# The head of a fused linear-attention and Mish kernel, rebuilt: roots on ScalarE, the wv load on ScalarE's queue, a value tile between fold and logits, eight PSUM banks, one ones column

## The chip, the cores and the metric

The kernel runs on one core of a Trainium2 chip. The metric is the device time of one execution in microseconds (us). Three runs of the kernel before took 184.01, 184.12 and 184.20 us; the median is 184.12.

The engines are called TensorE (PE in the profile; its weight loads are PEld), VectorE (DVE), ScalarE (ACT), GpSimd (POOL) and SyncE (SP). SP and ScalarE also issue the transfers (SPq, ACTq).

## The reference, cut to what matters

One input x of 2048 rows and 512 columns is normalised and goes into two branches, whose results are added to x.

```python
x = A_x
xn = _layernorm(x, axis=-1)
return x + _A_ref(xn, A_wqkv, A_w_phi, A_wo) + _B_ref(xn, B_w1, B_b1, B_w2)

def _A_ref(x, wqkv, w_phi, wo):                       # 32 heads of 16
    q, k, v = ...                                     # x @ wqkv, split
    pq = jnp.einsum("bhsd,hdf->bhsf", q, w_phi)
    pk = jnp.einsum("bhsd,hdf->bhsf", k, w_phi)
    phi_q = jnp.concatenate([_softmax(pq), _softmax(-pq)], axis=-1)
    phi_k = jnp.concatenate([_softmax(pk), _softmax(-pk)], axis=-1)
    kv = jnp.einsum("bhsf,bhsd->bhfd", phi_k, v)
    z  = jnp.einsum("bhsf->bhf", phi_k)
    num = jnp.einsum("bhqf,bhfd->bhqd", phi_q, kv)
    den = jnp.einsum("bhqf,bhf->bhq", phi_q, z)[..., None] + 1e-6
    return (num / den) @ wo                           # heads joined again

def _B_ref(x, w1, b1, w2):                            # F = 1792
    h = x @ w1 + b1
    return (h * jnp.tanh(softplus(h))) @ w2           # Mish
```

## The kernel before, in words

Rows are worked on in 16 tiles of 128, in four groups of four. Nothing is scheduled by a planner: the text of the kernel is the order of each engine's work (`manual_schedule`), and every engine takes its own list from the front. The order was written out by hand.

**The head** (L419 to L491) prepares the first group.

- Loads. SP's queue issues x tiles 0 and 1, the k part of wqkv turned by a DMA transpose (`wT`, `load_turned`, L90), x tiles 4 to 7, `wv`, `w1`, x tiles 8 to 15. ScalarE's queue issues `wsrc` (w_phi), x tiles 2 and 3, `b1b`.
- GpSimd builds `ident` and the block mask `block`; VectorE makes `KVmask` and the mask columns of `kvm` from it (L443 to L445).
- TensorE runs twelve matmuls on the identity (`warm`, L455) while nothing else can run.
- `ln_stats` (L116 to L122): VectorE takes the statistics of two tiles and aggregates them; GpSimd makes the reciprocal root from the variance (add, then power -0.5). `ln_apply` (L128) normalises on VectorE.
- `fold` (L98): TensorE multiplies `wT` with `Wbd`, the block-diagonal w_phi that VectorE builds (L461). The four slices of the result are evicted to `wkp`, three by ScalarE (L108), one by VectorE (L106).
- `ln_turn_pe` (L140): TensorE transposes a normalised tile into PSUM (`ptr`), one copy (L143) brings it to `xnT`.
- `logits(0, i)`: four matmuls `xnT` by `wkp` (L156), evicted to `p_sb` by ScalarE (L194). All four tiles' logits are done before the first `value(i)`, which multiplies by `wv` (L156) and is evicted to `vext` (L164).
- `extremes(0)` on VectorE (L207 to L218): maximum and minimum over each 16 of `p_sb`, and the differences `e`. In its middle it normalises tiles 4 to 7 and has their transposes done by DMA (L146).
- `hidden(5)`: five units of the first layer of the Mish branch, each four matmuls (L176) and one activation with the Mish table on ScalarE (L183). There are 56 such units in all, put between the other steps to fill TensorE.

**The loop over four groups**, s = 0 to 3: exponentials of `e` (L228, with a change of ScalarE's table before and after), `accumulate(s-1)` (L281: `pkv` += e' x `vext`, 32 matmuls), value and logit tiles of the next groups, `normalise` on VectorE (L246 to L259), more hidden units (6 + 11, 14, 8, 10), then `extremes(s+1)`. In group 0 three logit tiles go into one PSUM tile of three banks (`wide`, evicted at L531), and after that VectorE clears `pkv` (L533).

**After the loop:** the exponentials of the first query group, `accumulate(3)`, `mask_kv` (L294 to L307), and then per half group: `attend` (L325; evicted by ScalarE, L334 to L341), `combine` on VectorE (L357 to L382), a DMA transpose of its result `ob` (L385), `second_layer` (L398), `project_out` (L407), the residual and the store (L415, L416).

**PSUM** has eight banks. One pool of five (`ps`, tag `mm`) serves the matmul results of the head and of the loop; one of three banks (`ps2`) holds in turn `wide`, `pkv` and each `pnd` of `attend`.

`vext` holds, beside the 128 columns of v for eight heads, eight columns of ones (128 to 135), from which `pkv` gets the sums z in eight equal columns.

Of the kernel before, what the change touches and what calls it, by code (L numbers as in the profile page):

```python
# [17 lines left out]
def kernel(  # L18
# [12 lines left out]
    nc = tc.nc  # L31
    P = 128
    S, D, NH, DH, F = 2048, 512, 32, 16, 1792
    NG = 4
    TPG = 4
# [24 lines left out]
    ps2 = ctx.enter_context(tc.tile_pool(name="ps2", bufs=1, space=bass.MemoryType.PSUM))  # L60

    x_sb = persist.tile([P, NT, D], BF16, name="x_sb")
    xnT = persist.tile([P, NT, KT, P], BF16, name="xnT")
# [11 lines left out]
    wqp = wqk[:, :, 0:D]  # L75
    wo_sb = wqk[:, :, D : 2 * D]
    ident = consts.tile([P, P], BF16, name="ident")
    mhalf = consts.tile([P, TPG], FP32, name="mhalf")
    block = consts.tile([P, 8, 16], BF16, name="block")
    KVmask = consts.tile([P, 136], FP32, name="KVmask")  # L80
# [29 lines left out]
    def ln_stats(t0, n):  # L110

        stats = lnp.tile([P, TPG, nc.vector.BN_STATS_DIM], FP32, name="stats")
        mv = lnp.tile([P, TPG, nc.vector.BN_AGGR_DIM], FP32, name="mv")
        rstd = lnp.tile([P, TPG], FP32, name="rstd")
        for i in range(n):
            nc.vector.bn_stats(stats[:, i, :], x_sb[:, t0 + i, :])  # L116
        for i in range(n):
            nc.vector.bn_aggr(mv[:, i, :], stats[:, i, :])
        nc.gpsimd.tensor_scalar(
            out=rstd[:, 0:n], in0=mv[:, 0:n, 1], scalar1=1e-5, scalar2=None, op0=ALU.add  # L120
        )
        nc.gpsimd.tensor_tensor(out=rstd[:, 0:n], in0=rstd[:, 0:n], in1=mhalf[:, 0:n], op=ALU.pow)  # L122
        return mv, rstd

    def ln_apply(t0, n, mv, rstd, xn, at):
        engine = nc.gpsimd if t0 > TPG else nc.vector
        for i in range(n):
            engine.tensor_scalar(  # L128
                out=xn[:, at + i, :],
                in0=x_sb[:, t0 + i, :],  # L130
                scalar1=mv[:, i, 0:1],
                scalar2=rstd[:, i : i + 1],
                op0=ALU.subtract,
                op1=ALU.mult,
            )

    def ln_turn_pe(t, xn, i, copy):
        ptr = ps.tile([P, 512], BF16, name="ptr", tag="mm")
        for kt in range(KT):
            nc.tensor.transpose(  # L140
                ptr[:, kt * P : (kt + 1) * P], xn[:, i, kt * P : (kt + 1) * P], ident[:]
            )
        copy(xnT[:, t, :, :], ptr[:].rearrange("p (k c) -> p k c", k=KT))  # L143
# [18 lines left out]
    def value(t, copy):  # L162
        pv = project(wv, t)
        copy(  # L164
            vext[(t // TPG) % 2][:, t % TPG, :, 0:128], pv.rearrange("p (j c) -> p j c", j=4)
        )
# [108 lines left out]
    def accumulate(g):  # L275
        pkv = kv_of[0]
        e = e_of.pop(g)
        for j in range(4):
            for pl in range(2):
                for i in range(TPG):  # L280
                    nc.tensor.matmul(  # L281
                        blocks(pkv, pl, j, 136),
                        lhsT=e[:, i, pl, j * P : (j + 1) * P],
                        rhs=vext[g % 2][:, i, j, :],
                        start=False,
                        stop=(g == NG - 1 and i == TPG - 1),
                        skip_group_check=True,
                    )

    def mask_kv():  # L290
        pkv = kv_of[0]

        a, b = by_parts(pkv, 0, 136)
        nc.vector.tensor_tensor(  # L294
            out=kvm[:, :, 0:3, 0:136], in0=a,
            in1=KVmask[:, None, None, :].to_broadcast([P, 2, 3, 136]), op=ALU.mult,
        )
        nc.vector.tensor_tensor(
            out=kvm[:, :, 3, 0:136], in0=b,
            in1=KVmask[:, None, :].to_broadcast([P, 2, 136]), op=ALU.mult,  # L300
        )
        a, b = by_parts(pkv, 128, 136)
        nc.vector.scalar_tensor_tensor(
            out=kvm[:, 1, 0:3, 128:136], in0=a[:, 1], scalar=1e-6,
            in1=KVmask[:, None, 128:136].to_broadcast([P, 3, 8]), op0=ALU.add, op1=ALU.mult,
        )
        nc.vector.scalar_tensor_tensor(  # L307
            out=kvm[:, 1, 3, 128:136], in0=b[:, 1], scalar=1e-6,
            in1=KVmask[:, 128:136], op0=ALU.add, op1=ALU.mult,
        )  # L310

    nd_of, oT_of, po_of, tmp_of = {}, {}, {}, {}
# [103 lines left out]
        queue.dma_start(o_v[:, t, c], y)  # L416


    nc.sync.dma_start(x_sb[:, 0:2, :], x_v[:, 0:2, :])  # L419
    with nc.allow_non_contiguous_dma(reason="tiny w_phi load"):  # L420
        nc.scalar.dma_start(wsrc[:], wphi_v)
    wT = load_turned(D)
    nc.scalar.dma_start(x_sb[:, 2:4, :], x_v[:, 2:4, :])
    nc.scalar.dma_start(b1b[:], b1_v[:, :])
    nc.sync.dma_start(x_sb[:, 4:8, :], x_v[:, 4:8, :])
    nc.sync.dma_start(wv[:], wqkv_v[:, :, 2 * D : 3 * D])
    nc.sync.dma_start(w1_sb[:], w1_v[:, :, :])
    nc.sync.dma_start(x_sb[:, 8:16, :], x_v[:, 8:16, :])

# [13 lines left out]
    nc.vector.tensor_copy(KVmask[:, 0:P], block[:].rearrange("p h d -> p (h d)"))  # L443
    nc.vector.tensor_copy(KVmask[:, P : P + 8], block[:, :, 0])
    nc.vector.tensor_copy(  # L445
        kvm[:].rearrange("p l j c -> p (l j) c")[:, :, 136:144],
        block[:, None, :, 0].to_broadcast([P, 8, 8]),
    )
# [1 line left out]

    dve, act = nc.vector.tensor_copy, nc.scalar.copy

    warm = ps.tile([P, 4, P], FP32, name="warm", tag="mm")
    for _ in range(12):
        nc.tensor.matmul(  # L455
            warm[:], lhsT=ident[:], rhs=ident[:, None, :].to_broadcast([P, 4, P]),
            start=True, stop=True,
        )

    st0 = ln_stats(0, 2)  # L460
    nc.vector.tensor_tensor(  # L461
        out=Wbd[:].rearrange("p j (h e) -> p j h e", h=8),
        in0=block[:, None, :, :].to_broadcast([P, 4, 8, 16]),
        in1=wsrc[:, :, None, :].to_broadcast([P, 4, 8, 16]),
        op=ALU.mult,
    )
    st1 = ln_stats(2, 2)
    xn = lnp.tile([P, TPG, D], BF16, name="xn", tag="xn")
    ln_apply(0, 2, *st0, xn, 0)
    fold(wT, wkp, (3,))  # L470
    ln_turn_pe(0, xn, 0, dve)
    ln_turn_pe(1, xn, 1, act)
    pb = ps.tile([P, 512], BF16, name="pb", tag="mm")
    nc.tensor.transpose(pb[:, 0:FT], b1b[:], ident[0:FT, 0:FT])
    ln_apply(2, 2, *st1, xn, 2)
    logits(0, 0, act)
    for i in range(2, 4):
        ln_turn_pe(i, xn, i, dve)
    nc.vector.tensor_copy(b1f[:], pb[:, 0:FT])
    for i in range(1, TPG):  # L480
        logits(0, i, act)

    def normal(t0, st, xn):
# [6 lines left out]
    extremes(0, lambda: normal(TPG, st, xn))  # L490
    nc.sync.dma_start(w2_sb[:], w2_v[:, :, :])  # L491
    nc.sync.dma_start(wo_sb, wo_v[:, :, :])
    for i in range(TPG):
        value(i, act)
    hidden(5)

    for s in range(NG):
        exponentials(s, (0, 1) if s else (0,))
        if s > 0:
            accumulate(s - 1)  # L500
        if s < NG:
# [112 lines left out]
```

## Time and profile before

| | us |
|---|---|
| median of three runs | 184.12 |
| the profiled execution | 183.97 |
| its span in the profile | 182.3 |
| PE busy | 175.2 |
| DVE busy | 147.6 |
| ACT busy | 126.7 |
| POOL busy | 25.0 |

The span begins with the first instruction of the profile and ends with the last; 1.67 us of the execution lie outside of it. All times in the text are counted from the start of the span. "Busy" counts the time that an engine's instructions were being executed. Matmuls overlap in it: one of 512 columns is listed with some 379 ns, but in a stream they start 216 ns apart. "Waits" are idle times of an engine, put down to whatever was released last before the idle time ended. In a timeline row the first number is the start and the second the time to the end of the last instruction of the row; a bracket names the idle time before it and its releaser.

### The profile page before, as it was taken

What the parts mean: (1) busy time and instruction counts of PE and PEld (TensorE: products, weight loads), DVE (VectorE), ACT (ScalarE), POOL (GpSimd) and SP (SyncE); (2) the same over time, 40 slices, a digit from 0 to 9 for tenths busy, and PEclk for the clock granted to TensorE, in tenths of its full rate; (3) what the DMA queues carried; (4) which work ended last, traced back from release to release, by engine and by line L of the source; (5) the groups of instructions that cost most, each with busy time, mean ns of one, the idle gap of its engine ahead of it and who ended that gap; (6) DMA issues with size and microseconds to landing.
All of it is one profiled execution on the core that took longest, in us unless ns stands there. A gap on an engine that the chain in (4) does not pass through costs nothing.

```text
span 182.3 us, 2743 instructions
## 1 busy us (share of the span) xinstructions
PE 175.2 (96%) x1024; PEld 90.3 (50%) x1039; DVE 147.6 (81%) x255; ACT 126.7 (70%) x194; POOL 25.0 (14%) x30
## 2 busy tenths in 40 slices
PE   6799999999999999999999999999999999999993
PEld 2454344465444645564455455455554545455561
DVE  2989979998999899988999786299916997647963
ACT  2367999999998899979986889573842558235300
POOL 4403079300694000000000000000000000000000
PEclk9999999999999999999999999999999999999999
DMA  6998896300023600000000840963079401990633
GB/s 145 271 402 283 174 348 168 60 0 5 0 48 67 119 0 0 0 0 4 0 0 0 155 79 2 190 153 63 0 166 198 96 6 38 198 195 31 82 94 115
DMA packets 44393, 18.02 MB, mean 99 GB/s; under 512 B 36828, under 2 KB 43868, under 8 KB 44380
## 3 DMA queue, kind: packets, MB, share of 16 engines
q1 hardware_dynamic: 43408, 17.50, 40.5%
q10 hardware_dynamic: 972, 0.35, 0.7%
q8 instruction: 8, 0.13, 0.3%
q14 instruction: 5, 0.04, 0.1%
HBM read 6.84 MB, written 2.10 MB: 49 GB/s over the span
## 4 chain that ended last, share of the span: by engine, by line
PE 78%; DVE 9%; DMA 5%; ACT 4%; issue 1%; SPq 0%; DVEq 0%
PE po L398 22%; PE ph L176 22%; PE pproj L156 17%; PE po L407 7%; PE pkv L281 4%; PE pnd L325 4%; DMA wT<-in_A_wqkv_dram 3%; DVE stats L116 2%; ACT e L228 2%; DMA ob<-ob 2%; DVE m L207 1%; PE pfold L98 1%; DVE xn L128 1%; ACT L183 1%; DVE e L218 1%
## 5 line engine op out<-in xcount | busy, mean ns | idle before, releaser
L398 PE MATMUL po<-w_sb,acts 128*128 128x512 bf16 (+1 forms) x232 | 50.3, 366 | 0.3
L176 PE MATMUL ph<-xnT,w_sb 128*128 128x512 bf16 x224 | 49.5, 379 | 0.3 <-ACT acts L183 0.3
L183 ACT ACTIVATE acts<-ph,b1f 128x512 bf16<-128x512 f32 x56 | 35.3, 702 | 3.1 <-PE ph L176 3.0
L176 PEld LDWEIGHTS <-w_sb 128*128 128x128 bf16 x224 | 21.8, 98 | 26.7 <-issue 0.6
L228 ACT ACTIVATE e<-e 128x2048 bf16<-128x2048 bf16 x16 | 29.8, 1903 | 6.2 <-DVE e L218 6.1
L398 PEld LDWEIGHTS <-acts 128*128 128x128 bf16 x238 | 22.8, 98 | 22.0
L156 PEld LDWEIGHTS <-xnT 128*128 128x128 bf16 x192 | 18.3, 98 | 21.6 <-DMA xnT<-xn 0.8
L194 ACT CAST p_sb<-pproj 128x512 bf16<-128x512 f32 x25 | 13.7, 587 | 9.3 <-PE pproj L156 9.3
L415 DVE TENSOR_TENSOR x_sb<-po,x_sb 128x512 bf16<-128x512 f32 (+1 forms) x17 | 10.6, 654 | 11.4 <-PE po L407 11.4
L246 DVE TENSOR_REDUCE s<-e 128x128 f32<-128x2048 bf16 x8 | 18.2, 2277 | 1.9 <-ACT e L228 1.9
L128 POOL TENSOR_SCALAR xn<-x_sb,mv,rstd 128x512 bf16<-128x512 bf16 x8 | 16.7, 2102 | 0.2
L407 PE MATMUL po<-wqk,ob 128*128 128x512 bf16 (+1 forms) x66 | 14.7, 366 | 0.3
L156 PE MATMUL pproj<-wv,xnT 128*128 128x512 bf16 x61 | 14.8, 379 | 0.2
L156 PE MATMUL pproj<-wqk,xnT 128*128 128x512 bf16 x62 | 14.4, 379 | 0.1
L334 ACT CAST wkp<-pnd 128x768 bf16<-128x768 f32 x8 | 6.4, 798 | 11.3 <-PE pnd L325 7.4
L207 DVE TENSOR_TENSOR m<-m 128x512 bf16<-128x512 bf16 (+1 forms) x32 | 11.5, 359 | 1.1
L156 PE MATMUL pproj<-wkp,xnT 128*128 128x512 bf16 x50 | 11.8, 379 | 0.1
L207 DVE TENSOR_TENSOR m<-p_sb 128x1024 bf16<-128x1024 bf16 x16 | 10.9, 684 | 1.0 <-ACT p_sb L194 1.0
L325 PEld LDWEIGHTS <-qT 128*128 128x128 bf16 x128 | 9.1, 98 | 3.8
L116 DVE BATCH_NORM_STATS2 stats<-x_sb 128x6 f32<-128x512 bf16 x16 | 9.9, 678 | 1.1 <-DMA x_sb<-in_A_x_dram 1.1
L325 PE MATMUL pnd<-kvm,qT 128*128 128x144 bf16 x128 | 10.6, 226 | 0.0
L259 DVE TENSOR_TENSOR e<-e,r 128x2048 bf16<-128x2048 bf16 x8 | 10.2, 1281 | 0.3
(68 smaller groups left out, 176.4 us busy)
## 6 DMA issues: line engine op xcount, KB each, us to landing
w_sb<-in_B_w_dram SPq DMA_DIRECT2D x2, 1792.0 KB, 8.7
out_dram<-x_sb SPq DMA_DIRECT2D x15, 128.0 KB, 1.9
x_sb<-in_A_x_dram SPq DMA_DIRECT2D x1, 1024.0 KB, 11.7
x_sb<-in_A_x_dram SPq DMA_DIRECT2D x1, 512.0 KB, 4.5
wv<-in_A_wqkv_dram SPq DMA_DIRECT2D x1, 512.0 KB, 5.4
wqk<-in_A_wo_dram SPq DMA_DIRECT2D x1, 512.0 KB
x_sb<-in_A_x_dram SPq DMA_DIRECT2D x1, 256.0 KB, 3.1
x_sb<-in_A_x_dram ACTq DMA_DIRECT2D x1, 256.0 KB, 3.5
```

The lines of the kernel that those rows point to most:

```text
L116: nc.vector.bn_stats(stats[:, i, :], x_sb[:, t0 + i, :])
L128: engine.tensor_scalar(out=xn[:, at + i, :], in0=x_sb[:, t0 + i, :], scalar1=mv[:, i, 0:1], scalar2=rstd[:, i : i + 1], op0=ALU.subtract, ...
L156: nc.tensor.matmul(pp, lhsT=xnT[:, t, kt, :], rhs=w[:, kt, :], start=(kt == 0), stop=(kt == KT - 1),)
L176: nc.tensor.matmul(ph[:], lhsT=w1_sb[:, kt, f * P : (f + 1) * P], rhs=xnT[:, g * TPG : (g + 1) * TPG, kt, :], start=(kt == 0), stop=(kt == ...
L183: nc.scalar.activation(acts[:, f, g * 512 : (g + 1) * 512], ph[:], ACT.Mish, bias=b1f[:, f : f + 1])
L194: copy(p_of[s][:, i, :], pp)
L207: nc.vector.tensor_tensor(out=m[:], in0=src[:, :, 0:half], in1=src[:, :, half : 2 * half], op=op)
L228: nc.scalar.activation(v, v, ACT.Exp)
L246: nc.vector.reduce_sum(t[:], v.rearrange("p t l (c e) -> p (t l c) e", e=16), axis=AX.X)
L325: nc.tensor.matmul(blocks(pnd, pl, j, 144), lhsT=qT_of[h][:, i, pl * 4 + j, :], rhs=kvm[:, pl, j, :], start=True, stop=True,)
L398: nc.tensor.matmul(po[:, c], lhsT=acts[:, f, t * P : (t + 1) * P], rhs=w2_sb[:, f, c], start=(f == 0), stop=False,)
L407: nc.tensor.matmul(po[:, c], lhsT=oT_of[h][:, t % 2 * 4 + j, :], rhs=wo_sb[:, j, c], start=False, stop=(j == 3),)
```

## The change

The head is written anew, with smaller edits in the loop:

1. **Loads.** `wv` is issued by ScalarE after x tiles 2 and 3, in the place of `b1b`; `b1b` is issued by SP, in the place of `wv`.
2. **Roots.** For tiles 0 to 3 each tile has its own statistics, aggregate and root. The root is a `Sqrt` activation on ScalarE (with an `eps` tile as bias), followed by a reciprocal on VectorE. ScalarE first runs one root of `eps`.
3. **Order.** VectorE: statistics and normalising of tiles 0 and 1 interleaved, `Wbd` between them; then the statistics of 2 and 3. The four roots stand first in ScalarE's order. TensorE: transposes of tile 0, fold, transposes of tile 1, `value(0)`, `logits(0, 0)`, transposes of 2 and 3, b1, the other logits, the other values. All four fold slices are evicted by ScalarE, after its copy of tile 0's transposes; the other copies of `xnT` are VectorE's (1, 2) and ScalarE's (3). There are ten warm matmuls.
4. **PSUM.** The head has a pool of its own with three banks (`psh`: warm, `ptr`, `pb`) beside the five of `ps`; it is closed before `ps2` is opened over the same banks.
5. **Masks.** `KVmask` and `kvm`'s mask columns are made by GpSimd.
6. **Hidden units.** Six in the head instead of five, nine in group 3 instead of ten.
7. **pkv.** No memset; the first matmul into each bank starts it by its `start` flag. The matmuls use 129 columns (one of ones) instead of 136, and `mask_kv` spreads that column.

```diff
+    psh = head.enter_context(tc.tile_pool(name="psh", bufs=3, space=bass.MemoryType.PSUM))
...
     def accumulate(g):
-        pkv = kv_of[0]
+        if g == 0:
+            kv_of[0] = ps2.tile([P, 3, 512], FP32, name="pkv", tag="kv")
...
-                        blocks(pkv, pl, j, 136),
+                        blocks(kv_of[0], pl, j, 129),
                         lhsT=e[:, i, pl, j * P : (j + 1) * P],
-                        rhs=vext[g % 2][:, i, j, :],
-                        start=False,
+                        rhs=vext[g % 2][:, i, j, 0:129],
+                        start=(g == 0 and i == 0 and (j == 0 or (j == 3 and pl == 0))),
...
+    nc.gpsimd.memset(eps[:], 1e-5)
     nc.sync.dma_start(x_sb[:, 0:2, :], x_v[:, 0:2, :])
...
     nc.scalar.dma_start(x_sb[:, 2:4, :], x_v[:, 2:4, :])
-    nc.scalar.dma_start(b1b[:], b1_v[:, :])
+    nc.scalar.dma_start(wv[:], wqkv_v[:, :, 2 * D : 3 * D])
+    nc.scalar.activation(root[:], eps[:], ACT.Sqrt)
     nc.sync.dma_start(x_sb[:, 4:8, :], x_v[:, 4:8, :])
-    nc.sync.dma_start(wv[:], wqkv_v[:, :, 2 * D : 3 * D])
+    nc.sync.dma_start(b1b[:], b1_v[:, :])
...
-    for _ in range(12):
+    for _ in range(10):
...
+    def spread(t):
+        nc.vector.bn_stats(hstats[t][:], x_sb[:, t, :])
+    def root_of(t):
+        nc.vector.bn_aggr(hmv[t][:], hstats[t][:])
+        nc.scalar.activation(hrstd[t][:], hmv[t][:, 1:2], ACT.Sqrt, bias=eps[:])
+    def apply(t):
+        nc.vector.reciprocal(hrstd[t][:], hrstd[t][:])
+        nc.vector.tensor_scalar(out=xn[:, t, :], in0=x_sb[:, t, :], ...)
+    spread(0)
+    root_of(0)
+    spread(1)
+    apply(0)
+    root_of(1)
     nc.vector.tensor_tensor(out=Wbd[:]..., ...)
-    st1 = ln_stats(2, 2)
-    xn = lnp.tile([P, TPG, D], BF16, name="xn", tag="xn")
-    ln_apply(0, 2, *st0, xn, 0)
-    fold(wT, wkp, (3,))
-    ln_turn_pe(0, xn, 0, dve)
-    ln_turn_pe(1, xn, 1, act)
-    pb = ps.tile([P, 512], BF16, name="pb", tag="mm")
-    nc.tensor.transpose(pb[:, 0:FT], b1b[:], ident[0:FT, 0:FT])
-    ln_apply(2, 2, *st1, xn, 2)
-    logits(0, 0, act)
-    for i in range(2, 4):
-        ln_turn_pe(i, xn, i, dve)
+    apply(1)
+    spread(2)
+    root_of(2)
+    spread(3)
+    root_of(3)
+    ln_turn_pe(0, xn, 0, act)
+    fold(wT, wkp, ())
+    ln_turn_pe(1, xn, 1, dve)
+    apply(2)
+    apply(3)
+    value(0, act)
+    logits(0, 0, act)
+    ln_turn_pe(2, xn, 2, dve)
+    ln_turn_pe(3, xn, 3, act)
+    pb = psh.tile([P, 512], BF16, name="pb", tag="head")
+    nc.tensor.transpose(pb[:, 0:FT], b1b[:], ident[0:FT, 0:FT])
     nc.vector.tensor_copy(b1f[:], pb[:, 0:FT])
-    for i in range(1, TPG):
+    for i in range(1, 4):
         logits(0, i, act)
...
-    for i in range(TPG):
+    head.close()
+    ps2 = ctx.enter_context(tc.tile_pool(name="ps2", bufs=1, space=bass.MemoryType.PSUM))
+    for i in range(1, TPG):
         value(i, act)
-    hidden(5)
+    hidden(6)
...
-            kv_of[0] = ps2.tile([P, 3, 512], FP32, name="pkv", tag="kv")
-            nc.vector.memset(kv_of[0][:, :, 0:432], 0.0)
-        hidden((11, 14, 8, 10)[s])
+        hidden((11, 14, 8, 9)[s])
```

More of the change, by code (lines that the diff above doesn't have):

```diff
@@ L59 @@
     ps = ctx.enter_context(tc.tile_pool(name="ps", bufs=5, space=bass.MemoryType.PSUM))
-    ps2 = ctx.enter_context(tc.tile_pool(name="ps2", bufs=1, space=bass.MemoryType.PSUM))
+    head = ExitStack()
+    psh = head.enter_context(tc.tile_pool(name="psh", bufs=3, space=bass.MemoryType.PSUM))
     x_sb = persist.tile([P, NT, D], BF16, name="x_sb")
@@ L77 @@
     ident = consts.tile([P, P], BF16, name="ident")
+    eps = consts.tile([P, 1], FP32, name="eps")
+    root = consts.tile([P, 1], FP32, name="root")
     mhalf = consts.tile([P, TPG], FP32, name="mhalf")
@@ L137, in ln_turn_pe @@
     def ln_turn_pe(t, xn, i, copy):
-        ptr = ps.tile([P, 512], BF16, name="ptr", tag="mm")
+        ptr = psh.tile([P, 512], BF16, name="ptr", tag="head")
         for kt in range(KT):
@@ L290, in mask_kv @@
     def mask_kv():
-        pkv = kv_of[0]
-        a, b = by_parts(pkv, 0, 136)
+        a, b = by_parts(kv_of[0], 0, 128)
         nc.vector.tensor_tensor(
-            out=kvm[:, :, 0:3, 0:136], in0=a,
-            in1=KVmask[:, None, None, :].to_broadcast([P, 2, 3, 136]), op=ALU.mult,
+            out=kvm[:, :, 0:3, 0:128], in0=a,
+            in1=KVmask[:, None, None, 0:128].to_broadcast([P, 2, 3, 128]), op=ALU.mult,
         )
         nc.vector.tensor_tensor(
-            out=kvm[:, :, 3, 0:136], in0=b,
-            in1=KVmask[:, None, :].to_broadcast([P, 2, 136]), op=ALU.mult,
-        )
-        a, b = by_parts(pkv, 128, 136)
-        nc.vector.scalar_tensor_tensor(
[L304 to L309, printed above, removed]
+            out=kvm[:, :, 3, 0:128], in0=b,
+            in1=KVmask[:, None, 0:128].to_broadcast([P, 2, 128]), op=ALU.mult,
+        )
+        a, b = by_parts(kv_of[0], 128, 129)
+        for pl in range(2):
+            nc.vector.scalar_tensor_tensor(
+                out=kvm[:, pl, 0:3, 128:136], in0=a[:, pl].to_broadcast([P, 3, 8]), scalar=5e-7,
+                in1=KVmask[:, None, 128:136].to_broadcast([P, 3, 8]),
+                op0=ALU.add, op1=ALU.mult,
+            )
+        nc.vector.scalar_tensor_tensor(
+            out=kvm[:, :, 3, 128:136], in0=b.to_broadcast([P, 2, 8]), scalar=5e-7,
+            in1=KVmask[:, None, 128:136].to_broadcast([P, 2, 8]), op0=ALU.add, op1=ALU.mult,
         )
@@ L442 @@
         nc.gpsimd.memset(vext[i][:, :, :, 128:136], 1.0)
-    nc.vector.tensor_copy(KVmask[:, 0:P], block[:].rearrange("p h d -> p (h d)"))
-    nc.vector.tensor_copy(KVmask[:, P : P + 8], block[:, :, 0])
-    nc.vector.tensor_copy(
+    nc.gpsimd.tensor_copy(KVmask[:, 0:P], block[:].rearrange("p h d -> p (h d)"))
+    nc.gpsimd.tensor_copy(KVmask[:, P : P + 8], block[:, :, 0])
+    nc.gpsimd.tensor_copy(
         kvm[:].rearrange("p l j c -> p (l j) c")[:, :, 136:144],
@@ L451 @@
     dve, act = nc.vector.tensor_copy, nc.scalar.copy
-    warm = ps.tile([P, 4, P], FP32, name="warm", tag="mm")
-    for _ in range(12):
+    warm = psh.tile([P, 4, P], FP32, name="warm", tag="head")
+    for _ in range(10):
         nc.tensor.matmul(
@@ L458 @@
         )
-    st0 = ln_stats(0, 2)
+    xn = lnp.tile([P, TPG, D], BF16, name="xn", tag="xn")
+    hstats = [lnp.tile([P, nc.vector.BN_STATS_DIM], FP32, name=f"hstats{i}", bufs=1) for i in range(4)]
+    hmv = [lnp.tile([P, nc.vector.BN_AGGR_DIM], FP32, name=f"hmv{i}", bufs=1) for i in range(4)]
+    hrstd = [lnp.tile([P, 1], FP32, name=f"hrstd{i}", bufs=1) for i in range(4)]
+    def spread(t):
[5 more added lines that the diff above has]
+        nc.vector.reciprocal(hrstd[t][:], hrstd[t][:])
+        nc.vector.tensor_scalar(
+            out=xn[:, t, :], in0=x_sb[:, t, :], scalar1=hmv[t][:, 0:1], scalar2=hrstd[t][:],
+            op0=ALU.subtract, op1=ALU.mult,
+        )
+    spread(0)
[3 more added lines that the diff above has]
+    root_of(1)
     nc.vector.tensor_tensor(
```

## The prediction

> **What bounds the kernel now.** I read the busy times first, then who waited on TensorE, then the timeline of the first 30 us, then the waits of the middle. Page, part 1, and the waits of TensorE in the trace (who waited, for whom: us in total, times, longest):
>
> ```profile
> PE 175.2 (96%) x1024; PEld 90.3 (50%) x1039; DVE 147.6 (81%) x255; ACT 126.7 (70%) x194; POOL 25.0 (14%) x30
> ```
> ```profile
> PE warm L455 <- POOL ident masks.py:199: 1.4, 1, 1.4
> ...
> PE pfold L98 <- DMA wT<-in_A_wqkv_dram: 0.7, 1, 0.7
> ...
> PE ptr L140 <- DVE wkp L106: 0.6, 1, 0.6
> PE ph L176 <- ACT acts L183: 0.3, 1, 0.3
> PEld L407 <- DMA ob<-ob: 0.3, 1, 0.3
> ```
>
> TensorE (PE) is full. From the fold at 6.75 to 178.2 it stands still for little over a microsecond: 0.6 and some tenths in the head, 0.3 at 29.15, 0.3 at 115.6. So the head decides, and so do the two later waits, because they show chains on other engines that are as late as TensorE itself. The head, from the timeline (start, us, engine, line, operation, idle before it):
>
> ```profile
> 3.92 1.28 DVE L116 BATCH_NORM_STATS2 stats<-x_sb 128x6 f32<-128x512 bf16 x2 [1.12 <-DMA x_sb<-in_A_x_dram]
> 5.13 0.30 DVE L118 BATCH_NORM_AGGREGATE mv<-stats 128x2 f32<-128x6 f32 x2
> 5.34 0.39 DVE L461 TENSOR_TENSOR Wbd<-block,wsrc 128x512 bf16<-128x512 bf16 x1
> 7.06 0.71 DVE L128 TENSOR_SCALAR xn<-x_sb,mv,rstd 128x512 bf16<-128x512 bf16 x2
> 7.18 1.56 ACT L108 CAST wkp<-pfold 128x512 bf16<-128x512 f32 x3 [3.28 <-PE pfold L98]
> 8.46 0.41 DVE L143 COPY xnT<-ptr 128x512 bf16<-128x512 bf16 x1
> 9.02 1.04 PE L156 MATMUL pproj<-wkp,xnT 128*128 128x512 bf16 x4
> 16.39 3.83 PE L176 MATMUL ph<-xnT,w_sb 128*128 128x512 bf16 x17
> ```
>
> The reader is to see the handover: wkp is complete at 8.74, xnT of tile 0 at 8.87, the first logits start at 9.02, and `hidden` starts at 16.39. From there four rows carry a delay of the head to the end:
>
> ```profile
> 22.91 1.91 ACT L228 ACTIVATE e<-e 128x2048 bf16<-128x2048 bf16 x1
> 29.15 10.52 PE L176 MATMUL ph<-xnT,w_sb 128*128 128x512 bf16 x48 [0.35 <-ACT acts L183]
> 42.47 0.69 DVE L164 CAST vext<-pproj 128x512 bf16<-128x512 f32 x1 [0.66 <-PE pproj L156]
> 108.79 0.29 DVE L357 TENSOR_TENSOR u<-ds 128x128 f32<-128x128 f32 x1 [0.51 <-ACT ds L341]
> ```
>
> **The change, step by step.** *Who runs first on ScalarE.* The program order of the changed kernel puts four roots (one per tile) on ScalarE, then the copy of xnT tile 0, then all four wkp copies. ScalarE takes its work in order, so the xnT copy and the fold's copies stand behind the fourth root, and that waits for the fourth variance on VectorE. Queued behind it are also the value and logit evictions; TensorE waits for all of them.
>
> VectorE's list up to that variance, with rows of before (a dependent small step starts 0.03 after the end of the one before, as at 108.79 and 109.12; independent ones overlap by 0.07): statistics 0.68, aggregate 0.16, Wbd 0.39, normalise 0.40. A 128x1 reciprocal is not shown. The nearest are 0.55 for 128x64 and 0.35 for 128x32, which on a line give 0.16 (bounds 0.13, the shortest small copy, and 0.35). A 128x1 root is not shown either: 0.22 (128x32 copy) to 0.33 (with the 0.115 by which the biased 128x512 activation, 0.702, exceeds the plain cast, 0.587); I take 0.25. Then: statistics 0 from 3.92 to 4.60, aggregate to 4.76, statistics 1 to 5.36, reciprocal and normalise 0 to 5.89, aggregate 1 to 5.98, Wbd to 6.30, root 1 ready 6.29, reciprocal and normalise 1 to 6.88, statistics 2 to 7.49, aggregate 2 to 7.68, statistics 3 to 8.29, aggregate 3 to 8.48. Fourth root 8.51 to 8.76. Copy of xnT 0 (0.586; ScalarE's neighbours overlap by 0.1): done 9.27. Four wkp copies at 0.49 each (three took 1.56): first from 9.17, last done 11.23.
>
> *TensorE.* Transposes of tile 0 go into the idle time before the fold. Value tile 0 starts at 9.30 and ends at 10.16; the first logits run three of their four matmuls and wait for the last wkp slice until 11.26, ending 11.48 (0.216 per matmul, the spacing in the 10.52 us x48 row). Two tiles' transposes 0.45, b1's 0.06, twelve logit matmuls 2.59, twelve value matmuls 2.59: `hidden` starts at 17.17 against 16.39, **0.78 late**. The new banks do remove the 0.6 wait for a bank at 8.60. Late next is what is described above.
>
> *One hidden unit more in the head* (6, later 9 instead of 10). TensorE's total is unchanged, but ScalarE evicts six activations before the first exponential (22.91). Then follow exponential 1.91, p_sb 0.57, exponential 1.91, table 1.28, activation 0.70, and the restart of TensorE at 29.15, which waits for exactly this chain. One unit is 4 x 0.216 = 0.86: the restart moves by 0.78 + 0.86 = **1.64**.
>
> *Does it reach the end?* After 29.15 TensorE runs without a wait to the value tiles that VectorE waits for at 42.47 and again 0.17 at 43.33. From 43.94 VectorE and the exponentials wait only for one another (0.33 at 62.9, 1.18 at 80.5, 1.41 at 98.0 on ScalarE for e) or for TensorE work that is as late, up to `combine(0)` at 108.79 and the transfer of ob, which lands at 115.84. Off come 0.09 (32 pkv matmuls, below) and the 0.48 that VectorE waited for ScalarE's ds after its own work ended (108.28 to 108.79): ds would be ready at about 109.7, VectorE's extremes end at 109.9. So ob lands 1.64 - 0.09 - 0.48 = **1.07 late**. TensorE, with one unit less in stage 3, gets to `project_out(0)` earlier and waits. From there to 178.2 it never waits now, and the 1.07 stays.
>
> *Edits with one answer, nothing.* The three mask copies moved to GpSimd (0.37 + 0.24 + 0.13) ran while VectorE waited for x until 3.92, and GpSimd is idle from 2.7 to 5.5; without that cover they would cost at most 0.74. The memset of pkv (1.14) goes, but VectorE then waits 1.97 instead of 0.83 for the value tiles. mask_kv: one small step more (0.17) inside the 0.99 that VectorE waits for p_sb at 102.24. The flag adds no instruction. Ten warm matmuls still end before the fold.
>
> *Ones column:* pkv 136 to 129 columns. Rows: 32 matmuls in 1.89 = 59 ns; 16 fold matmuls of 128 in 0.89 = 56 ns; 144 columns 62 ns. I take 56, 0.09 for each of four groups; at worst 62 ns, 0.11 lost per group. Three of the four groups lie under VectorE's chain.
>
> *wv on ScalarE's queue.* wT's packets flow alone from 4.5 to 6.0 at 257 to 291 GB/s; wv's 524 KB now follow x tiles 2 to 3 on the other queue and meet them. Below: nothing, if the two share without loss. Above: 2.76 us, all of wv first at 190 GB/s, the slowest slice with a load under way. I take 1.5 (353 GB/s, the slice from 3.5 to 4.0 with most traffic on ScalarE's queue): fold at 8.25. This is hidden by the blocked ScalarE: the fold's first eviction is wanted 0.43 after its start, and ScalarE is free at 9.17, so up to 8.74 it costs nothing, beyond that it costs in full. b1b takes wv's place on SP's queue with 0.70 of issue instead of 0.50, and w1, x 8 to 15 behind it move 0.2; w1 is wanted at 17.2 and landed at 15.3. On this queue the Trainium skill ("DMA: Bandwidth & Descriptors", section "Issuing engines are not separate DMA queues") speaks against the change: transfers started by different engines run on the same 16 DMA engines and interleave. By that rule wT pays for every packet of wv that goes ahead of it; with the page's limit of about 358 GB/s from HBM per core that is an estimate of 1.5 us, a fold at 8.2, and a sum of 185.2 as well. The slice from 3.5 to 4.0, in which both queues moved packets, does not contradict it.
>
> **Sum.** 0.78 + 0.86 - 0.09 - 0.48 = +1.07 on the profiled execution (183.97, of which 182.3 is span): 185.04. The median shown is 0.15 above it: **185.2**.
>
> **Rivals.**
> *A, the block is shorter (faster).* If ScalarE is free when the fold's banks are (7.18), the logits end 9.6, `hidden` starts at 15.34, 1.05 early: -1.05 + 0.86 - 0.57 = -0.76, 183.4. It decides from `hidden` at 16.10, that is a fourth variance at 7.41 instead of 8.48. For it: aggregates began 0.07 before the recorded end of the statistics, not after. Against it: the sum of VectorE's steps even with all such overlaps is some 0.5 less, not 1.07. 0.15.
> *B, no change: the later chains give way.* If neither the restart at 29.15 nor ob at 115.84 binds, only TensorE's list counts: 0.78 - 0.37 (pkv) - 0.65 (both waits gone) = -0.24, 183.9. For it: the waits are only 0.3 each. Against it: VectorE is busy eight or nine tenths in nearly every slice of the page from 14 to 98 us. 0.11.
> *C, wT comes after 8.74.* All of wv first at 190 GB/s: fold at 9.51, +0.77 more, 186.0. 0.09.
> *D, the clock.* The warm matmuls start 0.43 apart until 5.23 and closer after it. If the gate closes in the thin stretch up to 9.3, some 3.9 us run at half pace, +1.95: 187.1. Speaking for it, the skill ("TensorE: Matmul & The Clock Gate", "Part 4: PE-mode transpose") says that transposes do not count as busy in the same way; by that rule the sum would be the 187.1 of this case; the row, in which the idle 0.7 before the fold did not close the gate, leaves it at 185.2. Its chance: 0.04.
>
> **Numbers.** My forecast 0.61, its own range 184.6 to 185.7: the overlaps (-0.5) and the longer small steps and an uncovered ds wait (+0.5). The range reaches to B and C, 183.8 to 186.1, and leaves out A and D, 0.19. Within 0.2% (0.37 us, about what a measurement of this kernel can tell from no change) lies B: 0.11; faster is A: 0.15; slower the rest: 0.74.
>
> **What would show it.** Right: fourth root ending near 8.8 with ScalarE idle before it, xnT's copy at 8.7, TensorE idle 8 to 9.3 and about 0.4 before the last wkp matmul of tile 0, `hidden` at 17.2, restart near 30.8, a wait for ob near 117. Wrong: a fold copy on ScalarE before 8, `hidden` before 16.4, a fold after 8.74, matmuls 0.43 apart after 9, or no wait for ob.

## The result, and the profile after

| us | before | after |
|---|---|---|
| median of six runs | 184.16 | **190.1** |
| lowest to highest | 183.97 to 184.23 | 185.88 to 190.81 |
| profiled execution | 183.97 | 185.88 |
| its span | 182.3 | 184.2 |

The change makes the kernel slower, by 5.9 us in the medians. The forecast was 185.2 with a range up to 186.1: the direction was right, the time was not. The six executions of after lie 4.9 us apart where those of before lie 0.26 apart. The ratio of 1.014 (95% interval 1.011 to 1.017) leaves out the four slow executions near 190, whose clock was lower; before_wv_act, below, takes as long in all six of its executions. The profiled execution is the fastest of the six. Its mean granted clock (the share of full speed at which TensorE was allowed to run) is 1.0; the four from 189.82 to 190.81 have 0.982. A microsecond at half clock loses half a microsecond, so that is 2 x 0.018 x 188.5 = 6.8 us at half clock.

Busy times (page, part 1) and the waits of TensorE in after:

```profile
PE 176.0 (96%) x1022; PEld 91.0 (49%) x1037; DVE 146.1 (79%) x254; ACT 128.6 (70%) x201; POOL 23.0 (13%) x30
```
```profile
ACT hrstd L476 <- DVE hmv L475: 4.0, 4, 1.5
...
PE warm L461 <- POOL ident masks.py:199: 1.4, 1, 1.4
...
PE pfold L101 <- DMA wT<-in_A_wqkv_dram: 1.4, 1, 1.4
...
PE ph L179 <- ACT acts L186: 0.5, 1, 0.5
PEld L411 <- DMA ob<-ob: 0.4, 1, 0.4
```

Three things answer to before. The wait for a bank at `ptr` is gone. The wait of the fold for wT has doubled, 0.7 to 1.4. The two later waits, behind which a delay of the head reaches the end, are a little longer. The first row is new: ScalarE stands for 4.0 us before its roots. The timeline of after, head and then middle:

```profile
4.07 0.69 DVE L472 BATCH_NORM_STATS2 hstats<-x_sb 128x6 f32<-128x512 bf16 x1 [4.07 <-DMA x_sb<-in_A_x_dram]
...
8.16 1.89 PE L101 MATMUL pfold<-Wbd,wT 128*128 128x128 bf16 x16 [1.44 <-DMA wT<-in_A_wqkv_dram]
...
8.78 0.30 ACT L476 ACTIVATE hrstd<-hmv,eps 128x1 f32<-128x1 f32 x1 [0.50 <-DVE hmv L475]
8.98 0.57 ACT L146 COPY xnT<-ptr 128x512 bf16<-128x512 bf16 x1
9.44 2.05 ACT L111 CAST wkp<-pfold 128x512 bf16<-128x512 f32 x4
...
10.27 1.30 PE L159 MATMUL pproj<-wv,xnT 128*128 128x512 bf16 x4
...
11.41 1.03 PE L159 MATMUL pproj<-wkp,xnT 128*128 128x512 bf16 x4
```
```profile
25.50 1.91 ACT L231 ACTIVATE e<-e 128x2048 bf16<-128x2048 bf16 x1
...
31.74 10.52 PE L179 MATMUL ph<-xnT,w_sb 128*128 128x512 bf16 x48 [0.48 <-ACT acts L186]
```

The queue on ScalarE is as forecast: fourth root to 9.08 (8.76 forecast), copy of xnT at 8.98 (8.7), last wkp at 11.49 (11.23); VectorE began 0.15 later, because x came later. New is the 1.89 of the fold: 16 matmuls 0.107 us apart, not 0.056, and value tile 0 after it begins at half pace as well. This is not a clock that fell but one that had not yet risen. The warm matmuls, first in before, then in after:

```profile
1.42 4.67 PE L455 MATMUL warm<-ident 128*128 128x512 bf16 x12 [1.42 <-POOL ident masks.py:199]
```
```profile
1.45 4.45 PE L461 MATMUL warm<-ident 128*128 128x512 bf16 x10 [1.45 <-POOL ident masks.py:199]
```

In before they start 0.427 apart at first and 0.216 apart from 5.49 on. In after all ten start 0.40 to 0.43 apart, and 0.216 is reached only at 10.98, within value tile 0. The granted clock of the profile reads 1.0 in both slow stretches, so only the spacing tells.

With this pace the first logits end at 12.28, `hidden` starts at 18.12, 1.73 after before's 16.39 (0.78 was forecast), the restart moves by 31.74 - 29.15 = 2.59 = 1.73 + 0.86, and `ob` lands at 117.74, 1.90 late; the execution is 1.91 longer. From `hidden` on, this execution passes its delay to the end as the prediction said. Two questions remain: what made the head another 0.95 late here, and what costs some 4 us more in the executions near 190.

### The profile page after: what moved, and what is told of

Same layout as the page of the kernel before. It is cut to its first block, busy times and chain, and to the rows that moved or that the text cites. A ratio compares the mean times of both kernels' runs of the same rounds, so it can differ in the third digit from the quotient of the medians.

```text
span 184.2 us, 2747 instructions
## 1 busy us (share of the span) xinstructions
PE 176.0 (96%) x1022; PEld 91.0 (49%) x1037; DVE 146.1 (79%) x254; ACT 128.6 (70%) x201; POOL 23.0 (13%) x30
## 3 DMA queue, kind: packets, MB, share of 16 engines
HBM read 6.84 MB, written 2.10 MB: 49 GB/s over the span
## 4 chain that ended last, share of the span: by engine, by line
PE 45%; DVE 37%; ACT 8%; DMA 5%; issue 3%; SPq 0%; DVEq 0%
PE po L402 20%; DVE m L210 7%; DVE s L249 7%; PE po L411 7%; PE pproj L159 7%; DVE e L221 6%; PE ph L179 6%; ACT e L231 6%; DVE e L262 4%; DMA wT<-in_A_wqkv_dram 4%; PE pnd L329 3%; DVE r L257 3%; DVE stats L119 2%; DMA ob<-ob 2%; DVE m L216 2%
## 5 line engine op out<-in xcount | busy, mean ns | idle before, releaser
L179 PEld LDWEIGHTS <-w_sb 128*128 128x128 bf16 x224 | 21.9, 98 | 26.8 <-issue 0.8
L419 DVE TENSOR_TENSOR x_sb<-po,x_sb 128x512 bf16<-128x512 f32 (+1 forms) x17 | 10.6, 655 | 11.3 <-PE po L411 11.3
L159 PE MATMUL pproj<-wv,xnT 128*128 128x512 bf16 x61 | 15.2, 384 | 0.2
L329 PE MATMUL pnd<-kvm,qT 128*128 128x144 bf16 x128 | 10.6, 226 | 0.2 <-ACT ds L345 0.2
L338 ACT CAST wv<-pnd 128x768 bf16<-128x768 f32 x8 | 6.3, 791 | 5.9 <-PE pnd L329 3.7
```

Of the source, the lines that this page charges most:

```text
L159: nc.tensor.matmul(pp, lhsT=xnT[:, t, kt, :], rhs=w[:, kt, :], start=(kt == 0), stop=(kt == KT - 1),)
L179: nc.tensor.matmul(ph[:], lhsT=w1_sb[:, kt, f * P : (f + 1) * P], rhs=xnT[:, g * TPG : (g + 1) * TPG, kt, :], start=(kt == 0), stop=(kt == ...
L329: nc.tensor.matmul(blocks(pnd, pl, j, 144), lhsT=qT_of[h][:, i, pl * 4 + j, :], rhs=kvm[:, pl, j, :], start=True, stop=True,)
```

## The experiments

Each median stands beside that of the kernel before, measured alongside. Three theories. **Clock**: ten warm matmuls are too few, TensorE idles before the fold, and its clock drops. **Load**: wv on ScalarE's queue delays wT beyond the 8.74 that the prediction found harmless. **Block**: the roots ahead of ScalarE's list cost more than forecast.

### Keep TensorE busy before the fold (keep_pe_busy)

```diff
-    for _ in range(10):
+    for _ in range(12):          # warm
...
     ln_turn_pe(0, xn, 0, act)
+    for _ in range(7): nc.tensor.matmul(warm...)   # a bank that nobody reads
     fold(wT, wkp, ())
```


> The changed kernel with twelve warm matmuls instead of ten and seven more matmuls on the identity between the transposes of tile 0 and the fold, in a bank that nothing reads; the work is otherwise the same. Clock theory: the ten warm matmuls (4.3 us) leave the clock gate shut or let it shut again, and that is what makes the executions of the changed kernel lie between 185.9 and 190.8. Then all executions here lie within 0.5 us of one another, fold matmuls start 0.056 apart, and the median is about 185.4: the time of the profiled execution less the 0.5 by which its first logits ended late. Rival, the wv load: its place on the other queue makes the executions differ; then the spread stays and the median stays near 190. Block theory (four roots ahead of the copies on ScalarE): 185.4 is still 1.2 above the kernel before.

Measured 189.41 (186.88 to 190.27) against 184.15: at most 0.7 of the 5.9 us, less than the spread. TensorE ran matmuls until 7.97 and then waited 3.42 for wT; the fold began at 11.40. The clock alone falls as the first cause: wT was late although TensorE was warm.

### The loads in their old places (wv_on_sp)

```diff
-    nc.scalar.dma_start(wv[:], ...)
+    nc.scalar.dma_start(b1b[:], b1_v[:, :])
...
-    nc.sync.dma_start(b1b[:], b1_v[:, :])
+    nc.sync.dma_start(wv[:], ...)
```


> The changed kernel with the loads of wv and b1b back in their old places. Load theory: the fold starts at 6.75 again instead of 8.16; since ScalarE is blocked by the roots until 9.0, the first wkp copy does not start before 9.4 and the profiled execution gains at most 0.3 against 185.9. If the load alone made the executions differ, they now agree within 0.5 us. Clock theory: TensorE has as little to do as before between 5.7 and 9.3, only its idle time lies elsewhere, so the executions still differ by some us (186 to 191).

Measured 186.84 (185.92 to 187.86) against 184.15. The fold is back at 6.72 and at full pace, and 3.3 of the 5.9 us are back. The executions still differ, though: three take 185.92 to 186.14 at a granted clock of 0.997 to 1.0, three take 187.54 to 187.86 at 0.989 to 0.991. So the load is not the only thing that makes them differ; the lower clock goes with the longer times, but none of those three left a trace. In the profiled execution (186.05) what remains is no longer wT:

```profile
PE pproj L159 <- DMA wv<-in_A_wqkv_dram: 2.7, 1, 2.7
```

Value tile 0, which the change put ahead of the logits, now waits for wv until 10.72. So the early value tile needs the early load, and the early load is what hurts.

### xnT ahead of two roots (xnT_before_roots)

```diff
     apply(1)
+    ln_turn_pe(0, xn, 0, act)
     spread(2); root_of(2); spread(3); root_of(3)
-    ln_turn_pe(0, xn, 0, act)
     fold(wT, wkp, ())
```


> The changed kernel with the transposes of tile 0 and their copy on ScalarE ahead of the roots of tiles 2 and 3. Block theory: the copy starts at 6.6 instead of 9.0, the first wkp copy at 9.0 instead of 9.4, so that the last ends at 11.0 instead of 11.5: 0.4 gained in an execution whose clock is as in the profiled one (185.5). Clock theory: nothing is changed in the thin stretch, so the median stays near 190 with a spread of several us.

Measured 190.35 (190.03 to 190.66) against 184.15. The copy moved to 6.45, and it helped nothing, since the fold began only at 12.10:

```profile
12.10 1.89 PE L101 MATMUL pfold<-Wbd,wT 128*128 128x128 bf16 x16 [5.69 <-DMA wT<-in_A_wqkv_dram]
```

### The kernel before with ten warm matmuls (before_ten_warm)

```diff
-    for _ in range(12):
+    for _ in range(10):
```


> The kernel before with ten warm matmuls instead of twelve, nothing else. Clock theory: TensorE then stands idle from 5.7 to 6.75, after 4.3 us of work instead of 4.7, and some executions get the full clock late: the executions differ, and the median rises by 0.5 to 5 us above 184.2. Rival (the clock has nothing to do with it; loads or the block on ScalarE make the loss): 184.2, all executions within 0.3 us.

Measured 184.08 (183.96 to 185.18) against 184.15, ratio 1.0008 [0.9994, 1.0022]: nothing in the median, so ten warm matmuls are not what costs 5.9 us. But two of the twelve executions took 185.14 and 185.18, at a granted clock of 1.0, where no execution of before in any of these comparisons took more than 184.79. A clock that rises late, as in the profiled execution of after, would look like that; neither of the two left a trace, so it is not shown.

### The kernel before with the loads exchanged and nothing else (before_wv_act)

```diff
-    nc.scalar.dma_start(b1b[:], b1_v[:, :])
+    nc.scalar.dma_start(wv[:], ...)
...
-    nc.sync.dma_start(wv[:], ...)
+    nc.sync.dma_start(b1b[:], b1_v[:, :])
```


> The kernel before with only the two loads exchanged: wv on ScalarE's queue, b1b on SP's. Load theory (wv in flight beside the transpose of wT makes wT late, by an amount that differs from execution to execution): the fold starts at 8.2 to 12 instead of 6.75, nothing in this kernel covers it, and the time is 185.5 to 190, median near 188, with a spread of over 1 us. Rival (the new order of the head or its roots make the loss and the spread): 184.2, spread under 0.4 us.

Measured **189.74** (189.37 to 191.84) against 184.07, ratio 1.033 [1.029, 1.036]. This one edit of the change, in the kernel before, costs nearly as much as the whole change (5.7 of 5.9 us), with a granted clock of 0.982 in five of six executions (0.970 in the slowest). Its timeline, and its windows of 2 us (start and end; length; busy time of PE, PEld, DVE, ACT and POOL with instructions in brackets; PEclk; DMA share; GB/s):

```profile
10.62 1.89 PE L98 MATMUL pfold<-Wbd,wT 128*128 128x128 bf16 x16 [4.70 <-DMA wT<-in_A_wqkv_dram]
...
21.92 4.48 PE L176 MATMUL ph<-xnT,w_sb 128*128 128x512 bf16 x20
```
```profile
6.00:8.00 2.00, 0.00 (x0) 0.00 (x0) 1.84 (x6) 0.00 (x0) 1.32 (x3) 1.00 1.25 229
8.00:10.00 2.00, 0.00 (x0) 0.00 (x0) 0.00 (x0) 0.00 (x0) 0.41 (x1) 0.60 1.08 255
10.00:12.00 2.00, 1.38 (x14) 1.38 (x15) 0.00 (x0) 0.73 (x2) 0.00 (x0) 0.50 1.05 385
12.00:14.00 2.00, 1.64 (x15) 1.26 (x14) 1.45 (x4) 0.92 (x3) 0.00 (x0) 0.50 1.03 405
14.00:16.00 2.00, 2.00 (x13) 1.03 (x14) 0.36 (x2) 0.88 (x2) 0.00 (x0) 0.69 1.05 377
```

TensorE stands still from 6 to 10.6 for wT; the clock falls to a half at about 8.4 and comes back at about 15.2. A window is 2 us long, and what its PEclk lacks to 1.00 counts double at half clock: 4 x (0.40 + 0.50 + 0.50 + 0.31) = 6.84 us at half clock. The fold is 10.62 - 6.75 = 3.87 late, and half pace makes 5.53 of it at `hidden` (21.92 against 16.39). The profiled execution ends 189.50 - 183.97 = 5.53 late: all of it arrives. A mean clock of 0.982 goes with this course in both profiled executions that have it (this one and xnT_before_roots), and the four executions of after near 190 have the same clock. That they went this way is concluded from it, since none of the four left a trace. A late wT does not always cost as much clock: in keep_pe_busy the fold began at 11.40 and the profiled execution has 0.991.

### Half of wv beside the transpose (before_half_wv)

```diff
     nc.scalar.dma_start(x_sb[:, 2:4, :], ...)
+    nc.scalar.dma_start(wv[:, 0:2], wqkv_v[:, 0:2, 2 * D : 3 * D])
     nc.scalar.dma_start(b1b[:], b1_v[:, :])
...
-    nc.sync.dma_start(wv[:], ...)
+    nc.sync.dma_start(wv[:, 2:4], wqkv_v[:, 2:4, 2 * D : 3 * D])
```


> The kernel before with the first half of wv (256 KB) issued by ScalarE behind x tiles 2 and 3, ahead of b1b; the second half stays at wv's old place on SP's queue. Load theory by amount: half of the bytes beside wT's transpose give about half of the delay that before_wv_act shows (fold at 10.6): a fold near 8.7, 186 to 187. If any second stream beside the transpose harms in full, 189; if only the bytes beyond wT's own time harm, 184.2 to 185.

Measured 189.61 (188.03 to 190.21) against 184.02. Half the bytes do all of the harm, so the delay is not the time that wv's bytes take. b1b stayed on ScalarE's queue here, so its move is not the cause either:

```profile
10.61 1.89 PE L98 MATMUL pfold<-Wbd,wT 128*128 128x128 bf16 x16 [3.92 <-DMA wT<-in_A_wqkv_dram]
```

The transfers show how. The DMA view from 3.5 to 12.5 us, 40 slices of 0.225 us each, and the median us from issue to landing: before, then three with wv beside the transpose (after, before_wv_act, xnT_before_roots).

```profile
GB/s 372 344 312 278 216 271 289 279 281 291 286 142 83 96 182 150 259 232 296 391 378 373 396 391 378 396 412 432 360 385 414 382 446 382 398 414 398 430 382 414
...
wT<-in_A_wqkv_dram SPq DMA_TRANSPOSE x1, 5.4
```
```profile
GB/s 327 382 355 282 276 236 290 333 364 347 364 364 364 364 364 310 290 344 373 246 341 328 364 350 417 319 446 462 303 510 255 510 430 335 510 255 510 398 366 510
...
wT<-in_A_wqkv_dram SPq DMA_TRANSPOSE x1, 6.8
```
```profile
GB/s 378 374 340 285 220 271 305 355 216 177 283 299 305 263 250 244 198 191 222 105 121 129 143 223 329 333 332 346 418 274 299 457 410 340 478 319 446 398 398 446
...
wT<-in_A_wqkv_dram SPq DMA_TRANSPOSE x1, 9.3
```
```profile
GB/s 385 372 278 254 212 158 149 124 31 83 23 98 127 124 134 115 121 126 133 262 309 275 240 234 220 189 187 284 391 288 348 347 346 341 333 416 314 416 336 461
...
wT<-in_A_wqkv_dram SPq DMA_TRANSPOSE x1, 10.7
```

Before, the transpose runs at 216 to 291 GB/s and is done at the eleventh slice. In the profiled execution of after the two streams share: together they move 236 to 364 GB/s, and wT lands 1.4 later for it. In the late ones the total itself falls: to 105 to 143 GB/s in four slices of before_wv_act, and to 23 to 158 for 14 slices, some 3.2 us, in xnT_before_roots. There the two do not merely share the engines, both slow down. (The lowest slices of the other two late profiles are 92 in keep_pe_busy and 94 in before_half_wv.) The Trainium skill ("DMA: Bandwidth & Descriptors", section "Issuing engines are not separate DMA queues") has such transfers interleave on the same 16 engines. The profile of after agrees; the four late ones show that a second queue beside a transpose can also take bandwidth away.

### wv on ScalarE's queue, but later (wv_act_later)

```diff
-    nc.scalar.dma_start(wv[:], ...)              # after x tiles 2, 3
...
     root_of(1)
+    nc.scalar.dma_start(wv[:], ...)              # now behind the second root
```


> The changed kernel with wv still issued by ScalarE, but after its second root (at about 6.5 instead of 1.9). Load theory: wv then meets only the end of wT's transfer; the fold starts near 6.75, the executions agree within 0.5 us, wv lands near 10, and the block on ScalarE leaves 185.4. If it is ScalarE's queue itself that harms, whenever it is used, the fold is late and the executions differ as in the changed kernel.

Measured 193.99 (193.12 to 195.28) against 184.07, the slowest of all, where 185.4 was expected. The fold is on time at 6.62, but wv, issued at 6.1 beside w1 (1792 KB) on the other queue, takes 10.4 to land:

```profile
PE pproj L159 <- DMA wv<-in_A_wqkv_dram: 8.6, 1, 8.6
```

Value tile 0 starts at 16.52. In order on SP's queue wv landed 5.3 after its issue (wv_on_sp).

### Roots and order alone (roots_and_order), and with TensorE kept busy (roots_order_filled)

To price the block, wv stands in its old place and value tile 0 behind the logits; everything else of the change stays. The second kernel adds two warm matmuls, and nine behind the transposes of tile 1, into a bank that nobody reads.

```diff
     ln_turn_pe(1, xn, 1, dve)
+    for _ in range(9): nc.tensor.matmul(warm...)   # second kernel only
     apply(2); apply(3)
-    value(0, act)
     logits(0, 0, act)
...
-    for i in range(1, TPG):
+    for i in range(TPG):
         value(i, act)
```


> The changed kernel with wv and b1b loaded as before and value tile 0 back behind the logits; roots, masks, banks, pkv and the hidden units as changed. Load theory: the fold starts near 6.75 in all executions, which agree within 0.4 us. Block theory (the copy of xnT 0 and the fold's evictions stand behind the fourth root on ScalarE): xnT's copy at 9.0, last wkp copy at 11.5, first logits end 11.75, hidden starts near 17.4, and the time is 185.3 (1.2 above before). If the block is hidden somewhere, 184.3 or less.

> The kernel of roots_and_order (old loads, value tile 0 behind the logits) with twelve warm matmuls and nine more matmuls on the identity, into a bank that nothing reads, between the transposes of tile 1 and the first logits, where TensorE stood idle from 7.8 to 10.1; the work is otherwise the same. If the clock gate shuts because TensorE has too little to do there, it stays open now: logit matmuls 0.216 apart, executions within 0.4 us, and what is left is the block alone: 185.3 (1.2 above before). If the block costs all of the 187.0 by itself, the time stays at 186.2 to 187.8.

Measured 187.04 (186.17 to 187.79) against 184.07, and **186.11** (186.00 to 186.19) against 184.02. Of the first, the wait of TensorE and its windows:

```profile
PE pproj L159 <- ACT wkp L111: 2.1, 1, 2.1
```
```profile
8.00:10.00 2.00, 0.01 (x1) 0.10 (x1) 1.89 (x7) 1.50 (x5) 0.00 (x0) 1.00 1.10 378
10.00:12.00 2.00, 1.58 (x5) 0.46 (x5) 0.09 (x1) 1.49 (x4) 0.00 (x0) 0.85 1.01 403
12.00:14.00 2.00, 2.00 (x12) 1.23 (x12) 1.28 (x4) 1.17 (x2) 0.00 (x0) 0.50 1.02 410
14.00:16.00 2.00, 1.78 (x8) 0.81 (x8) 1.97 (x7) 0.75 (x2) 0.00 (x0) 0.79 1.06 354
```

Nothing here waits for wT. TensorE waits 2.08 for the copies behind the fourth root, and the clock is lost afterwards: 4 x (0.15 + 0.50 + 0.21) = 3.4 us at half clock. Of the five executions one kept a granted clock of 1.0, and it took 186.17. With the stretch filled, the five executions agree within 0.2 us, and the chain from `hidden` to the end is clean:

```profile
18.37 5.34 PE L179 MATMUL ph<-xnT,w_sb 128*128 128x512 bf16 x24
...
31.99 0.38 PE L179 MATMUL ph<-xnT,w_sb 128*128 128x512 bf16 x1 [0.51 <-ACT acts L186]
```
```profile
114.80 3.20 DMA ob<-ob
...
118.04 1.90 PE po L411 x8
```

`hidden` +1.98, restart 31.99 - 29.15 = +2.84 = 1.98 + 0.86, ob +2.15 (landing 117.99), time +2.09. So this order, with the hidden unit that moved, costs 2.1 us while the clock stays open, and the lost clock 0.9 more (187.04 against 186.11). With a value tile in the gap, as the change has it, and wv there in time, `hidden` would be 0.86 sooner, which makes about 185.25 by the same chain: worked out, not run.

### The evictions between the roots (roots_between)

```diff
-    def fold(wT, dst, dve):
+    def fold(wT, dst, dve, kts=range(4)):        # kts: the slices to do now
...
     apply(1)
+    ln_turn_pe(0, xn, 0, act)
+    fold(wT, wkp, (), (0, 1))
     spread(2); root_of(2)
+    fold(wT, wkp, (), (2,))
     spread(3); root_of(3)
-    ln_turn_pe(0, xn, 0, act)
-    fold(wT, wkp, ())
+    fold(wT, wkp, (), (3,))
```
This is roots_and_order with another order on ScalarE.

> The kernel of roots_and_order with ScalarE's order changed: copy of xnT 0, two fold evictions, root of tile 2, one eviction, root of tile 3, the last eviction. Block theory: xnT's copy at 6.5 instead of 9.0, the last wkp copy ends near 9.8 instead of 11.5, first logits end near 10, hidden starts near 16.5, the clock stays open since TensorE is never idle for long: 184.5, executions within 0.4 us. If other parts of the new head (reciprocals, all four evictions on ScalarE, six hidden units) cost as much by themselves, it stays above 185.

Measured 184.34 (184.21 to 184.64) against 184.02, ratio 1.0017 [1.0008, 1.0026]:

```profile
6.64 0.59 ACT L146 COPY xnT<-ptr 128x512 bf16<-128x512 bf16 x1 [0.28 <-PE ptr L143]
...
8.97 0.59 ACT L111 CAST wkp<-pfold 128x512 bf16<-128x512 f32 x1
```

With the same roots, the same evictions and other places in the queue, the copy comes 2.3 earlier than in after, the last wkp 1.9, and 2.7 of the 3.0 us that roots_and_order lost are gone: 1.8 against the filled kernel (186.11), the rest the clock, which is 1.0 in all twelve executions. The roots themselves are cheap; standing behind them is not.

### The rest of the change (before_banks_pkv), and xnT first (before_banks_xnT_first)

The first is the kernel before with edits 4, 5 and 7 (own banks for the head, masks on GpSimd, `pkv` without memset and with 129 columns). The second also has VectorE copy xnT of tile 0 before the fold's slice 3.

```diff
+    psh = head.enter_context(tc.tile_pool(name="psh", bufs=3, space=bass.MemoryType.PSUM))
...
-    fold(wT, wkp, (3,))
+    pf3 = fold(wT, wkp, (3,))                    # second kernel: returns its bank
     ln_turn_pe(0, xn, 0, dve)
+    dve(wkp[:, 3, :], pf3[:])
```


> The kernel before with the parts of the change that leave its loads, roots, order and hidden units alone: the head's own three PSUM banks, the masks on GpSimd, pkv started by a flag and 129 columns wide. If VectorE's and ScalarE's chain up to the transfer of ob sets the time, most of what TensorE saves in pkv is waited away: 183.9 to 184.1. If TensorE's list alone counts: 0.37 less, 183.8. A loss would show a cost of the odd width or of the flag that the rows did not show.

> The kernel of before_banks_pkv with one exchange on VectorE: the copy of xnT tile 0 ahead of the eviction of wkp slice 3. The copy's wait (TensorE stood idle 0.6 before the first logits) goes; the last slice is late only for the fourth matmul. First logits end near 9.2 instead of 9.7, all logits 0.4 to 0.5 earlier, which VectorE's chain passes on: 183.3, against 183.75.

Measured 183.75 (183.49 to 184.01), ratio 0.9982 [0.9973, 0.9991], and 183.63 (183.29 to 184.10), ratio 0.9976 [0.9966, 0.9986]. Both are faster than the kernel before, by 0.2%. In the first, the wait for a bank is gone and another stands in its place:

```profile
PE pproj L157 <- DVE xnT L144: 0.6, 1, 0.6
```

In the second the logits start at 8.49 instead of 8.85, but then tiles 2 and 3 are normalised later, and `hidden` gains only 0.2 (16.01 against 16.21). The 183.3 expected was missed; the intervals of the two overlap, so the second step is not told apart from nothing.

## Why the prediction was wrong, step by step

- **"wv on ScalarE's queue" failed.** The prediction bounded it by "nothing" and 2.76 us, took 1.5 with the fold at 8.25, and held that up to 8.74 it costs nothing, so the sum has no term for it. The 8.16 of the profiled execution agrees: there the two streams do share, at 236 to 364 GB/s together. But that is the one profile of five in which they do; that the profiled execution was this one is luck. In the other four with this load early, the fold begins at 10.61, 10.62, 11.40 and 12.10, that is 3.9 to 5.35 late, and the load alone costs 5.7 us (before_wv_act). The upper bound assumed that the engines go on moving at least the 190 GB/s of the slowest busy slice; in these four, slices fell to 105, 94, 92 and 23. Half the bytes doing the same harm shows that bytes over a rate was the wrong kind of sum for them.
- **The clock was priced as a rival, apart from the load.** Case D gave 1.95 us at 0.04, for a thin stretch up to 9.3. A stretch like it, up to 10.08, does lose the clock in roots_and_order (0.9 us in the median), and late wT makes a longer one: 4.70 idle in before_wv_act, where half clock adds 5.53 - 3.87 = 1.66. Case C (wT after 8.74) had the cause, at 0.09, but capped it at 9.51 and 186.0 and did not join it to D: in three of the four late profiles some 6.8 us at half clock follow, in keep_pe_busy 3.4.
- **"Who runs first on ScalarE" was right**, within about 0.3 us at each step. The fourth variance came 0.26 later: 0.15 because x came later, 0.11 because VectorE's small steps were longer.
- **TensorE's sum in the head was mis-sized** even where the load did little: first logits 12.28, not 11.48, mostly because the fold, the transposes of tile 1 and the start of value tile 0 ran at half pace. The sum put full pace there without a reason of its own, and ten warm matmuls at nothing. In this execution the clock had not risen after them; in before_ten_warm they cost nothing in the median and two executions of twelve took 1.1 us more. Whether twelve would have raised it here is not shown.
- **"Does it reach the end?" was right.** Restart = `hidden` + 0.86 in after and in roots_order_filled; recovered on the way were 0.69 in both, where the prediction had 0.09 + 0.48 = 0.57.
- **The other edits costed at nothing** were right: banks, masks and `pkv` together -0.3 us (before_banks_pkv), in which the 0.6 wait for a bank became a 0.6 wait for xnT. The forecast of 185.2 is close to what the change would cost without the load's harm (185.25 above, worked out and not run).
- **Rivals A and B** are out: in the fastest execution `hidden` started at 18.12, where A needed 16.10, and the restart and ob both passed the delay on, which B denied.

Open: why a transpose and a plain load slow each other so far below what either reaches alone, and why in the fastest execution of after they did not. A different load, or the transpose from another place, was not tried.

## What to carry to other kernels

A load moved to a second queue is not priced by its bytes: ask what is in flight beside it, and try that one line alone, because a late first operand can also leave TensorE idle long enough to lose its clock. On an engine that works in order, put the evictions that TensorE waits for ahead of small steps that wait for another engine; here that order was worth 2.7 us with the same roots and evictions, 0.9 of it the clock. Edits that need each other (an early value tile and an early wv) are tested as a pair, and a fastest execution far below the median says that a profile of it does not show what most executions do.

## What the runs showed of the hardware

- A DMA transpose of 512 KB that lands in 5.4 us alone took 6.8 to 10.7 us with 256 or 512 KB of plain load beside it on another queue.
- A 512 KB load issued beside 1792 KB of another queue took 10.4 us; in order on that queue it took 5.3.
- Matmuls of 512 columns started 0.427 us apart until 5.23 in before and until 10.70 in after, while the granted clock of the profile read 1.0; later they started 0.216 apart.
- Half-clock stretches came as 3.4 us (roots_and_order), 6.84 us (before_wv_act) and, in wv_act_later, from 11.7 to 21.9, as 10.2 us. The Trainium skill ("TensorE: Matmul & The Clock Gate", section "Part 1: The HAM clock gate (the "warmup" mystery)") gives a free-running window of 3413 ns, which agrees: they are one, two and three of it. It also asks for about an idle window before the clock drops; in the profiled execution of roots_and_order 2.08 us of TensorE's waiting was enough, and the measurement decides.
